# Constants in written order, the first batch's keys turned by TensorE, fillers at the end, and new instruction sequences

## The chip, the cores and the metric

The kernel runs on one core of one Trainium2 chip. The metric is device time in microseconds (us), the median of three runs. Five engines work beside each other: TensorE (PE) multiplies matrices, VectorE (DVE), ScalarE (ACT) and GpSimd (POOL) work on tiles element by element, and SyncE (SP) issues most of the DMA transfers. Each engine takes its instructions strictly in the order in which they were written for it. So an instruction that waits holds up everything queued behind it on its engine. Matrix products land in PSUM, everything else lies in SBUF.

## What is computed

Four batches of 12288 queries attend to pooled keys. The keys and values are one array: kv, averaged over 4 x 4 patches and multiplied by w_sr, 768 rows of 128 per batch. The 49152 rows that come out go through a layer of 8 experts, of which each row takes the one with the largest gate logit.

```
kv_pool = kv.reshape(B, H//r, r, W//r, r, C).mean(axis=(2, 4))     # r = 4
k = v = kv_pool.reshape(B, -1, C) @ w_sr
s = scale * (q @ k.T);  a = softmax(s);  x = a @ v
e = argmax(x @ w_gate);  p = softmax(x @ w_gate)[e]
out = p * (relu(x @ w1[e]) @ w2[e])
```

## The kernel before

**Blocks.** The rows are worked in 96 blocks of 512 queries, 24 to a batch (`block(t)`, from L1125). A block first makes three pairs of score products on PE (tile `s`, "scores"). For each pair ACT makes the exponential (L1166, tile `e`) and DVE the difference 1 + s - exp(s) (L1168, tile `r`). Then PE makes four groups of "values" (tile `po`): r times the keys in tile `v16`, and the query times the square M of the keys, which makes up for the terms taken out of r. The result goes, split into two half-precision parts, through a DMA transpose to tile `x`. The expert's products follow: `hidden` (x times `w1U`, tile `b`), ACT's relu, and `rows` (x times `L` and g times `w2U`), DVE's scaling by the gate (L1297, tile `y`) and the store.

**Keys.** `keys(b)` (from L528) makes a batch's keys. For the first batch kv is loaded by SP in 8 transfers of 512 KB and 8 of 256 KB; DVE adds pairs of rows ("joins", L603 and, for the last third, L565), PE sums the rest and turns it (the products `s<-ident,kv`, "key sums"), multiplies by w_sr, and ACT writes `vT` (keys down the partitions). From `vT` come the scaled keys `KT` for the scores, the centred keys `kt` (L698), and two turned copies: `v16`, and `kr` as a high and a low half-precision part. Here POOL makes the halves (L712, L714) and the copy `kp2` (L706), and SP turns them by two DMA transposes (L716 into `kr`, shown as PU, and L708 into `v16`). `square` multiplies `kr` by itself for M; nothing of the values can start without M and v16. The loads of the first batch borrow the buffers of `e`, `raw` and `r`.

**Expert.** `expert(b)` (from L748) guesses the batch's expert from the mean key, loads its two weight matrices and folds, sorts and packs them in a long chain over all engines that starts from the square of the keys (`Ms`). `hidden` and `rows` need its results w1U, zb, L and w2U. Until then blocks can only do scores and values.

**Constants.** Before all this some dozens of small tiles are made by DVE and POOL (L400 to L469). The counting row `iota_i` is made by POOL in a buffer called `e2`, the third buffer of `e`. These lines stand outside `tc.manual_schedule()`, so their place among the other instructions is chosen by the framework and not by the order in the file.

**Order.** All other work is handed to a planner (`Plan`, `op`, `order`, `issue`) as ops with an engine, an estimated duration and what they need and give. The order on each engine is written out by hand as lists of op numbers (`ORDER`), and `WAYS` chooses between variants of an op that different engines can do. The planner's estimated times decide two things only: which buffer an op gets, and where PE gets "fillers". A filler is three products of the constant `slots16` with itself (128 x 384 each) into a free PSUM bank, of no use for the result; it is put where the planner sees PE idle between 9 and 110 us.

**General steps.** After each of the first three batches a step with loads, a search and an indirect gather (`general_step`) is mixed in among the blocks; a loop at the end runs as many more as are left.

Of the kernel before, what the change touches and what calls it, by code (L numbers as in the profile page):

```python
# [17 lines left out]
P = 128  # L18
POOL = 4
# [65 lines left out]
PE 1 0 2 4-5 3 6-7 9-10 8 11 110 12 112 14 98-99 113 111 101 100 16 13 145 21 144 15 17 146 115-117 114 122-123 103 102  # L85
104-105 124 148 22 18 147 149-150 133 24 135 126 23 125 134 127-128 155 157 138-139 19 136 156 137 29 20 166 30 158-159 167
161 160 28 168 26 179 25 27 178 119 118 170 177 129 120 172 171 188 130 169 189 121 131 190 182 108 107 181 183 180 106 199
151 201 132 193 153 200 191-192 210 194 152 109 211 140 212 205 204 31 141 221 32 202-203 184 162 222-223 143 142 213-214
232 216 173 215 234 154 233 163 224 185 227 226 225 243 164 186 244 235 237 236 245 238 206 255 195 33 256 249 34 246 254
187 248 174 265 175 247 35 266 165 176 260 196 267 259 207 258 257 197 276 198 278 269 208 218 270-271 277 217 268 209 37  # L90
# [3 lines left out]
359 358 399 307 297 50 377 51 388 316 48 390 317 49 401 383 308 327 381 328 400 318 380 382 319 410 389 338 329 405 403-404  # L94
402 412 360 411 339 391-392 394 393 421 330 423 416 414 422 361 413 415 341 432-433 362 427 424-425 349 426 384 52 434 443
53 363 350 437 340 444 435 385 364 436 445 351 438 395 456 352 396 454 447-448 446 455 386 449 467 387 406 465 417 365 458
466 407 460 397 457 459 478 408 477 398 470 428 476 468 419 469 471 54 499 418 409 55 498 429 481-482 430 368 487 480 489
# [3 lines left out]
516 557 61-63 517 577 569 528 567 570 576 518 568 586 519 540 587 578 529 538 588 581 67 597 580 579 527 539 599 591 589 598  # L101
590 592 610 68 64 601 530 69 609 608 602 550 603 549 600 70 619-620 551 541 612 561 611 560 621 630 562 552 613-614 631 573
563 632 65 623-624 654 571 622 572 625 66 655 582 656 633 636 635 665 583 634 574 666 73-74 593 667 72 657 584 659 594 658
689 71 687 660 585 688 604 670 668 605 671 669 595 678 596 615 676 607 606 698 691 617 677 692-693 690 637 699 616 700 628
681 627 680 682 679 618 639 710 709 704 638 701 75 703 626 711 76 720 640-641 702 673 629 732 722 661 683 712-713 662 721
# [5 lines left out]
794 856 858 795 857 863 785 796 806 886 867 875 804 91 805 876 87 868 866 816 869 92 887 817 885 807 815 879-880 93 838 877  # L111
896 878 818 898 891 827 889 897 88 826 890 888 828 89 909 908 837 829 900 848 901 931-932 850 840 902 95 899 907 839 94 933
96 849 954 860 911-912 861 910 913 97 953 859 851 870 935 942 937 871 955 881 872 934 936 944 862 964 892 873 943 957 882
965 883 959 903 893 958 956 966 884 946-947 975 945 894 948 976 895 977 969 916 967 970 905 968 914-915 988 986 904 978 981
938 979 918 917 987 980 939 906 940 997 999 991-992 961 960 989 998 990 962 1019 941 1020 949 963 1010 919 1000 1009 1002
951 1003 950 1008 971 1001 993 973 1021 952 1030 1012 1011 972 983 1013-1014 1032 984 1031 1024 982 1025 1022 922 920 1041
974 1043 1023 921 995 1042 1033 1065 1036 994 1034-1035 1004 1063 985 1064 1044 996 1052 1045 1054 1047 1005 923 1046 1006
924 1017 1053 1069 1066 1007 1016 925 1074 1015 1067 1075 1068 926 1076 1057-1058 927 929 1056 1085 1055 1018 1080 1086 1070
# [6 lines left out]
ACT 0 2-3 1 4 6 5 7 112 9 114 10 8 103-104 115 113 106 105 14 19 11 18 12 138 137 13 139 116-117 121-122 21 108 107 20 123  # L125
15 22 140 128 141 130 16 129 124 17 145 147 23 132 146 28 131 152-153 29 148 27 154 25 162 24 133 26 161 118-119 160 125 120
168 156 126 155 169 127 170 110-111 163 109 175 142 177 176 144 182 143 171 183 134 184 30 135 189 31 178 165 149 164 191
190 197 136 157 185 199 150 198 166 192 204 151 205 167 206 200 179 212 32 213 33 211 172 158-159 219 207 193 220 173 221
# [226 lines left out]
def attention_moe(ctx: ExitStack, tc, q, kv, w_sr, w_gate, w1, w2, out):  # L355
# [90 lines left out]
    for i, n in enumerate(LIMITS):  # L446
        nc.vector.memset(limits[:, i:i + 1], float(2 * n - F + 1))
# [1283 lines left out]
```

## Time and profile before

| | |
|---|---|
| median of three runs | 735.5 us (734.69, 735.5, 737.92) |
| the profiled execution | 739.06 us, of which its span is 737.3 us |
| PE / DVE / ACT / POOL busy | 96% / 85% / 82% / 74% |
| products on PE, of them fillers | 7903, 66 |
| granted TensorE clock over the span | 0.995 |

The span runs from the first to the last instruction. The share of busy time is an average: the stages at the start, where PE waits for the first keys, and at the end look different from the middle. Matrix products are pipelined, so the shown time of one is longer than the distance from one to the next.

### The profile page before, as it was taken

To read this page: it belongs to the slowest core of one execution; us is meant where nothing else is said; L and a number is where in the kernel's file an instruction comes from. 1 tells how busy PE (TensorE), PEld (TensorE's weight loads), DVE (VectorE), ACT (ScalarE), POOL (GpSimd) and SP (SyncE) were. 2 spreads that over 40 slices of the span, in tenths; PEclk is the share of its full clock that TensorE was granted. 3 is DMA by queue.
4 is the path that set the end of the run, shared out by engine and by line. 5 is a ranking of instruction groups with operands and counts; after the bars stand their busy time and mean duration, and the time that the engine had idled before them with its cause. 6 is when DMAs were issued, how large, how long until landed. Compare 5 with 4: busy or idle time off the path is not lost.

```text
span 737.3 us, 20803 instructions
## 1 busy us (share of the span) xinstructions
PE 705.2 (96%) x7903; PEld 555.2 (75%) x7903; DVE 626.0 (85%) x1257; ACT 607.4 (82%) x1118; POOL 544.8 (74%) x777
## 2 busy tenths in 40 slices
PE   4999999999999998999999999999999999999995
PEld 4677777888777777787877777888877877877773
DVE  5679879889998997888998898898988899777874
ACT  0567888999888996889978888889989898798972
POOL 0376899886889878677778879878676787668752
PEclk9999999999999999999999999999999999999998
DMA  8797899995899999789789999979787899877532
GB/s 315 207 248 125 207 206 224 186 206 130 175 252 232 238 243 211 152 212 186 131 205 220 208 253 222 189 164 223 146 155 170 167 188 186 177 154 157 99 91 73
DMA packets 326757, 138.84 MB, mean 188 GB/s; under 512 B 212558, under 2 KB 318162, under 8 KB 326656
## 3 DMA queue, kind: packets, MB, share of 16 engines
q1 hardware_dynamic: 325904, 137.14, 85.3%
q8 instruction: 62, 1.02, 0.6%
q14 instruction: 39, 0.32, 0.1%
q10 hardware_dynamic: 560, 0.20, 0.1%
q0 software_dynamic: 192, 0.17, 0.1%
HBM read 59.12 MB, written 26.94 MB: 117 GB/s over the span
## 4 chain that ended last, share of the span: by engine, by line
PE 79%; DVE 9%; ACT 5%; DMA 3%; issue 2%; POOL 1%; SPq 0%; DVEq 0%; ACTq 0%; POOLq 0%
PE b L477 36%; PE po L477 24%; PE s L477 17%; DVE r L1168 4%; ACT e L1166 2%; DMA x<-xp 1%; ACT g L1272 1%; DVE xp L1203 1%; DMA kv<-in_kv_dram 1%; DVE y L1297 1%; DMA qT<-qp 1%; PE s L876 0%; ACT xp L1202 0%; POOL g L1262 0%; PE s L838 0%
## 5 line engine op out<-in xcount | busy, mean ns | idle before, releaser
L1168 DVE SCALAR_TENSOR_TENSOR r<-s,e 128x1024 bf16<-128x1024 f32 x288 | 346.0, 1215 | 38.8 <-ACT e L1166 37.0
L1166 ACT ACTIVATE e<-s 128x1024 f32<-128x1024 f32 x288 | 293.4, 1029 | 38.4 <-PE s L477 34.3
L477 PE MATMUL po<-v,r 128*128 128x145 f16 x2304 | 254.2, 228 | 2.5 <-DVE xp L1203 1.7
L477 PEld LDWEIGHTS <-r 128*128 128x128 bf16 x2304 | 168.2, 98 | 22.7 <-DVE xp L1203 1.6
L477 PE MATMUL s<-qT,KT 128*128 128x512 f16 x576 | 168.0, 379 | 5.7 <-DVE r L1168 3.7
L477 PE MATMUL b<-x,w1U 128*128 128x512 f16 x465 | 142.6, 379 | 3.0 <-DVE y L1297 2.6
L1272 ACT ACTIVATE g<-b,zb 128x512 f16<-128x512 f32 x185 | 128.0, 694 | 17.4 <-PE b L477 16.2
L477 PE MATMUL po<-M,qT 128*128 128x136 f16 x1152 | 131.5, 223 | 0.0
L477 PE MATMUL b<-w2U,g 128*128 128x128 f16 x1180 | 129.7, 220 | 0.0
L1264 POOL TENSOR_TENSOR g<-X,g 80x512 f16<-80x512 f32 x94 | 108.8, 1159 | 26.0 <-ACT g L1272 8.8
L477 PE MATMUL b<-L,x 128*128 128x128 f16 x1116 | 123.7, 220 | 1.6 <-DVE X L1252 1.3
L1149 POOL TENSOR_TENSOR qp<-qr,qp 128x512 f16<-128x512 f32 x94 | 108.7, 1161 | 13.5 <-DVE PU L939 3.5
L477 PEld LDWEIGHTS <-qT 128*128 128x128 f16 x1152 | 84.9, 98 | 30.0 <-issue 5.5
L477 PEld LDWEIGHTS <-x 128*128 128x128 f16 x1116 | 81.6, 98 | 18.1 <-issue 2.4
L1147 POOL CAST qp<-qr 128x512 f16<-128x512 f32 x94 | 57.1, 614 | 36.6 <-DVE r L565 22.2
L477 PEld LDWEIGHTS <-g 128*128 128x128 f16 x1180 | 82.9, 99 | 0.2 <-DVE g L1255 0.2
L1262 POOL CAST g<-X 128x512 f16<-128x512 f32 x94 | 57.5, 612 | 28.8 <-PE b L477 9.0
L477 PEld LDWEIGHTS <-KT 128*128 128x128 bf16 x576 | 51.1, 99 | 35.1 <-issue 11.8
L618 POOL TENSOR_TENSOR kv<-kv,kv 128x512 f32<-128x512 f32 x54 | 68.1, 1276 | 10.0 <-DMA kv<-in_kv_dram 3.7
L1297 DVE TENSOR_TENSOR y<-b,gt 128x512 f32<-128x512 f32 (+1 forms) x97 | 65.5, 678 | 8.6 <-PE b L477 4.7
L1260 ACT ACTIVATE X<-b,zb 128x512 f32<-128x512 f32 x94 | 65.1, 695 | 7.1 <-PE b L477 6.2
L477 PEld LDWEIGHTS <-w1U 128*128 128x128 f16 x480 | 45.6, 99 | 31.6 <-issue 2.4
(380 smaller groups left out, 921.5 us busy)
## 6 DMA issues: line engine op xcount, KB each, us to landing
qr<-in_q_dram SPq DMA_DIRECT2D x96, 256.0 KB, 3.4
out_dram<-y SPq DMA_DIRECT2D x95, 256.0 KB, 3.2
kv<-in_kv_dram SPq DMA_DIRECT2D x41, 512.0 KB, 5.7
raw<-in_moe_w_dram SPq DMA_DIRECT2D x14, 512.0 KB, 4.9
e<-in_kv_dram SPq DMA_DIRECT2D x3, 512.0 KB, 6.5
v_dram<-vT SPq DMA_DIRECT2D x4, 384.0 KB, 4.1
qT<-qp SPq DMA_TRANSPOSE x94, 3.9
x<-xp SPq DMA_TRANSPOSE x91, 3.9
```

The lines of the kernel that those rows point to most:

```text
L477: return nc.tensor.matmul(o, l, r, start=start, stop=stop)
L618: nc.gpsimd.tensor_add(flat(to), flat(to), flat(of))
L1147: op("POOL", .62, lambda: nc.gpsimd.tensor_copy(qp.tile[:, 0], qr.tile), T - 1.9 * LEN, [("qr", t)], [("qh", t)], [qr, qp])
L1149: op("POOL", 1.17, lambda: nc.gpsimd.tensor_sub(qp.tile[:, 1], qr.tile, qp.tile[:, 0]), T - 1.8 * LEN, [("qh", t)], [("qp", t)], [qr, qp])
L1166: op("ACT", 1.03, lambda e=e, ps=ps: nc.scalar.activation(e.tile, ps.tile, AF.Exp), at + .6, [("s", t, s)], [("e", t, s)], [ps, e])
L1168: op("DVE", 1.22, lambda e=e, ps=ps, s=s: nc.vector.scalar_tensor_tensor(r.tile[:, 2 * s:2 * s + 2], ps.tile, 1.0, e.tile, op0=ALU.add, op ...
L1203: op("DVE", .69, lambda: nc.vector.tensor_tensor(xp.tile[:, 1], po.tile[:, :, :C], xp.tile[:, 0], op=ALU.subtract), A + .5, [("xh", t)], [ ...
L1260: op("ACT", .69, lambda ph=ph, zu=zu: nc.scalar.activation(gf.tile, ph.tile, AF.Relu, bias=zu()), at + .5, [("ph", t, u), ("zb", b)], [("g ...
L1262: op("POOL", .62, lambda: nc.gpsimd.tensor_copy(gg.tile[:, 0], gf.tile), at + 1.5, [("gf", t)], [("gh", t), ("g", t)], [gf, gg])
L1264: op("POOL", 1.16, lambda: nc.gpsimd.tensor_sub(gg.tile[:PAIRS, 1], gf.tile[:PAIRS], gg.tile[:PAIRS, 0]), at + 2, [("gf", t), ("gh", t), ( ...
L1272: op("ACT", .78, lambda u=u, ph=ph, zu=zu: nc.scalar.activation(gg.tile[:, u], ph.tile, AF.Relu, bias=zu(), accum_out=k["fl"].tile[:, u - ...
L1297: nc.vector.tensor_tensor(y.tile[:, cs], py.tile.rearrange("p (c d) -> p c d", d=C)[:, cs], bc(gr["gt"].tile[:, 0, js], C)[:, cs], op=ALU. ...
```

## The change

Five things change.

1. The constants are put inside `tc.manual_schedule()`: they are issued in the order in which they are written, ahead of all the planner's work. No constant is added or taken away.
2. For the first batch the two turned copies are made by PE instead of DMA. `turn` transposes `vT` and `kt` by six products each into PSUM; ACT copies the one, scaled, into `v16` and the other into the high half of `kr`; DVE subtracts for the low half. POOL's three ops and SP's two transposes of this batch are gone. The other three batches keep the old way.
3. Fillers are allowed in two stretches of planned time: 9 to 110 us as before, and 690 to 800 us.
4. The planner's estimate of the 256 KB loads goes from 0.64 to 0.73 us.
5. All five lists of ORDER are new, and WAYS differs in 58 names. On PE there are two more ops (the turns), on DVE five more, on ACT as many as before, on POOL seven and on SP two fewer. Of the 96 blocks, 91 instead of 89 leave out the third part of `rows` (u); 20 instead of 22 give the split of x to POOL rather than DVE (x); 33 instead of 32 copy the logits on DVE (l); KT's second third goes from ACT to DVE (k1).

The first numbers of the lists, old and new, decoded: on DVE of before the joins start with op 2 (rows 0 and 1 of the first third), of after with ops 0 and 1 (the gate weights' scale), then 3 (rows 2 and 3), then 2. On PE of before the key sum of rows 0 and 1 (op 1) is first and the gate weights' product (op 0) second; of after the gate weights come first, then the sum of rows 0 and 1, then that of rows 2 and 3. On PE of after `turn` of vT is 13, `turn` of kt 14, `square` 15, the gate guess 16, the logits' product 17, the expert's first products 18 and 19; blocks 0 and 1 start at 100 and 112 (98 and 110 before). On DVE of after 181 and 176 are the query halves of blocks 1 and 0, 182 to 184 and 177 to 179 their `r`, 201 one of block 4; 18 is KT, 19 and 20 are kt, 21 the subtraction for kr, 22 M's low half, 23 to 25 the expert guess, 26 the logits.

```diff
 ORDER = turns("""
-PE 1 0 2 4-5 3 6-7 9-10 8 11 110 12 112 14 98-99 113 111 101 100 16 13 145 21 144 15 17 146 115-117 114 122-123 103 102
+PE 0-2 4-5 3 6-7 9-10 8 11 112 13 114 12 100 16 101 115 14 113 103 15 147 17-18 102 23 119 117 146 118 116 19 105 148 104
...
-DVE 2 0 3 5 1 6 8-10 12 7 13 4 11 14-16 179 17 21 18 22 19 181 174-175 182 180 177 176 23 20 42 199 24 198 25-26 200 183 27
+DVE 0-1 3 2 5-6 8-10 12-13 7 4 11 15 14 18 16 181 17 183 23 19 24 20 177 184 176 21 182 25 179 22 201 26 44 178 200 185
...
-SP 3 0-1 4 2 5 7 6 10 14 8 12 9 11 13 15 82 71 94 68 74 83 78 86 19 17 16 21 20 98 110 90 75 22 102 18 23 87 79 72 106 95 91
+SP 3 1-2 0 5 4 7 6 10 12 8 14 11 9 15 13 72 69 80 76 66 73 84 92 81 17 88 18-19 21 20 100 112 16 104 77 70 96 85 93 82 89 74
...
-            if o.eng == "PE" and self.filler and start < self.filler_end:
+            if o.eng == "PE" and any(lo < free["PE"] and start < hi for lo, hi in self.filler_times):
                 make, fill, us = self.filler
-                while free["PE"] > self.filler_start:
+                while True:
...
-    ident = keep("ident", [P, P])
-    make_identity(nc, ident)
+    with tc.manual_schedule():
+        ident = keep("ident", [P, P])
+        make_identity(nc, ident)
...
+        if b == 0:
+            back = {}
+            for name, of, needs in (("tv", vT, [("vT", b)]), ("tk", kt, [("kt", b)])):
+                to = back[name] = pair()
+
+                def turn(to=to, of=of):
+                    flat = to.tile.rearrange("p b x -> p (b x)")
+                    for t in range(KT):
+                        nc.tensor.transpose(flat[:, t * P:(t + 1) * P], of.tile[:, t * P:(t + 1) * P], ident)
+
+                op("PE", .68, turn, at + 3, needs, [(name, b)], [of, to])
+            keys_of = lambda n: back[n].tile.rearrange("p b x -> p (b x)")[:, :NK].rearrange("p (t c) -> p t c", c=P)
+            op("ACT", .83, lambda: nc.scalar.activation(v16.tile[:, :, :P], keys_of("tv"), AF.Copy, scale=cn[:, 11:12]), at + 4,
+               [("tv", b), ("rest", b)], [("v16", b)], [back["tv"], v16])
+            op("ACT", .83, lambda: nc.scalar.copy(kr.tile[:, 0], keys_of("tk")), at + 4.5, [("tk", b)], [("kr0", b)],
+               [back["tk"], kr])
+            op("DVE", .95, lambda: nc.vector.tensor_tensor(kr.tile[:, 1], keys_of("tk"), kr.tile[:, 0], op=ALU.subtract), at + 5,
+               [("kr0", b)], [("kr", b)], [back["tk"], kr])
+        else:
...
-    plan.filler, plan.filler_start, plan.filler_end = (bank().make, fill, .487), 9.0, 110.0
+    plan.filler, plan.filler_times = (bank().make, fill, .487), ((9.0, 110.0), (690.0, 800.0))
```

## Rows read from the trace of the kernel before

**Rows 1.** Busy time of PE, PEld, DVE, ACT, POOL; granted clock; DMA, in stretches.

```profile
500.00:600.00 100.00, 100.00 (x1187) 79.63 (x1185) 89.49 (x168) 90.47 (x168) 74.96 (x114) 1.00 0.87 170
715.00:737.30 22.30, 12.72 (x142) 9.87 (x139) 11.29 (x49) 6.76 (x16) 6.81 (x19) 0.90 0.20 60
```

**Rows 2.** The page's chain that ended last, by engine.

```profile
PE 79%; DVE 9%; ACT 5%; DMA 3%; issue 2%; POOL 1%; SPq 0%; DVEq 0%; ACTq 0%; POOLq 0%
```

**Rows 3.** Timeline of the first sums: start, length, engine, line, tiles, what was awaited.

```profile
8.30 1.22 DVE L603 TENSOR_TENSOR kv<-kv,kv 128x1024 f32<-128x1024 f32 x1 [6.18 <-DMA kv<-in_kv_dram]
...
9.67 3.75 PE L477 MATMUL s<-ident,kv 128*128 128x128 f32 x16 [9.67 <-DVE kv L603]
...
15.60 3.86 PE L477 MATMUL s<-ident,kv 128*128 128x128 f32 x32
```

**Rows 4.** What SP's queue waited for before 60 us: total, times, longest.

```profile
SPq L545 <- DVE slot L431: 5.1, 1, 5.1
```

**Rows 5.** Busy time in two stretches, with the DMA rate (GB/s) last.

```profile
9.00:12.00 3.00, 2.33 (x11) 2.36 (x12) 3.00 (x27) 0.00 (x0) 0.00 (x0) 1.00 1.04 415
12.00:15.00 3.00, 2.94 (x14) 2.06 (x14) 2.96 (x8) 0.00 (x0) 0.00 (x0) 1.00 0.89 288
```

**Rows 6.** Timeline from the centred keys to the first values, and L716's landing.

```profile
30.89 0.54 DVE L698 TENSOR_SCALAR kv<-vT,con 128x512 f32<-128x512 f32 x1
...
34.15 2.71 SPq L716 DMA_TRANSPOSE PU<-kv  x1
...
40.54 1.17 PE L477 MATMUL b<-PU 128*128 128x128 f16 x18
...
49.04 0.23 PE L477 MATMUL po<-v,r 128*128 128x145 f16 x1
...
DMA to landing us min/median/max: 5.1/5.1/5.1
```

**Rows 7.** Busy time in three stretches of the start.

```profile
28.00:40.00 12.00, 10.16 (x57) 5.49 (x57) 10.54 (x20) 7.74 (x10) 8.11 (x12) 1.00 0.96 214
40.00:46.00 6.00, 5.74 (x50) 3.97 (x47) 2.78 (x13) 5.30 (x10) 3.16 (x5) 1.00 1.02 312
46.00:60.00 14.00, 13.28 (x147) 11.66 (x147) 12.77 (x22) 8.12 (x13) 8.61 (x14) 1.00 0.92 183
```

**Rows 8.** Groups by line, 28 to 60 us: count, busy, mean ns, idle before.

```profile
L1168 DVE SCALAR_TENSOR_TENSOR r<-s,e 128x1024 bf16<-128x1024 f32 x11 | 13.4, 1219 | 1.0 <-ACT e L1166 0.8
L477 PE MATMUL b<-slots 128*128 128x384 f16 x45 | 9.3, 325 | 0.2
L838 PE MATMUL s<-ident,raw 128*128 128x128 f32 x8 | 1.1, 279 | 0.3 <-DVE r L1168 0.3
L845 ACT COPY kv<-s 128x1024 f32<-128x1024 f32 x1 | 1.0, 1012 | 0.8 <-PE s L838 0.8
L841 DVE TENSOR_TENSOR kv<-s,kv 128x768 f32<-128x768 f32 x1 | 1.0, 959 | 0.0
```

**Rows 9.** First and last products with w1U: count, ns, first and last start.

```profile
L477 PE MATMUL b<-x,w1U x465: 376/379/634, 82.1 to 724.2; 128*128 128x512 f16 x155
```

**Rows 10.** Busy time in a stretch of the end (clock third from last).

```profile
727.00:730.00 3.00, 2.73 (x34) 2.67 (x33) 1.25 (x6) 0.00 (x0) 0.00 (x0) 0.63 0.02 5
```

**Rows 11.** Chain that ended last, at the end.

```profile
725.96 3.25 PE b L477 x32
...
729.46 1.53 PE b L477 x25
```

**Rows 12.** PE's longest wait from 720 us on: total, times, longest.

```profile
PE b L477 <- DVE X L1252: 1.3, 1, 1.3
```

**Rows 13.** Busy time around the slowest stretch of the middle.

```profile
265.00:280.00 15.00, 13.89 (x155) 10.60 (x154) 13.26 (x24) 11.48 (x23) 10.05 (x15) 1.00 1.10 232
280.00:295.00 15.00, 13.56 (x143) 10.81 (x143) 11.94 (x21) 10.69 (x17) 14.79 (x16) 0.89 1.15 236
```

**Rows 14.** Chain that ended last, in that stretch.

```profile
271.96 8.90 DMA x<-xp
```

More of the change, by code (lines that the diff above doesn't have):

```diff
@@ L246, in __init__ @@
     def __init__(self, slots):
-        self.ops, self.slots, self.filler, self.filler_start, self.filler_end = [], slots, None, 0.0, 0.0
+        self.ops, self.slots, self.filler, self.filler_times = [], slots, None, ()
     def op(self, eng, us, fn, at, needs=(), gives=(), bufs=(), lands=0.0, moves=0.0, lock=False, way=None):
@@ L411, in attention_moe @@
-    col_i = keep("col_i", [P, NF], I32)
-    nc.gpsimd.iota(col_i, pattern=[[P, NF]], base=0, channel_multiplier=1)
-    iota_e = keep("iota_e", [P, E])
-    lists = keep("lists", [P, NL])
-    nc.vector.tensor_scalar_add(lists, iota_i[:, :NL], 1.0)
-    nc.vector.tensor_scalar_add(iota_e, iota_i[:, :E], float(-E))
-    slots16 = keep("slots16", [P, UN], F16)
-    own_at, used_at = OWN_U * P + OWN_AT, P + PAIRS
-    for lo, hi, n in ((0, P, 1), (P, used_at, USED + 1), (used_at, own_at, P + 1),
-                      (own_at + OWN, 2 * P, P + 1 + own_at - used_at), (2 * P, UN, RU - P + 1)):
-        nc.vector.tensor_scalar_add(slots16[:, lo:hi], iota_i[:, lo:hi], float(n - lo))
@@ L422, in attention_moe @@
-    nc.vector.memset(slots16[:, own_at:own_at + OWN], -1.0)
-    wg_raw = keep("wg_raw", [P, E])
-    wsr = keep("wsr", [P, C])
-    wg_st = keep("wg_st", [P, 4])
-    code = keep("code", [P, NJ + 1])
-    nc.vector.memset(code, 0.0)
-    left, steps = keep("left", [P, NL]), keep("steps", [P, NL])
-    nc.vector.memset(left, 0.0)
-    slot = keep("slot", [P, P + 1])
-    nc.vector.tensor_copy(slot, iota_i[:, :P + 1])
-    part_i = keep("part_i", [P, 1], I32)
-    nc.gpsimd.iota(part_i, pattern=[[0, 1]], base=0, channel_multiplier=1)
@@ L434, in attention_moe @@
-    part_col = keep("part", [P, 1])
-    nc.vector.tensor_copy(part_col, part_i)
-    own = keep("own", [P, UH + OWN])
-    nc.vector.memset(own, 0.0)
-    for i in range(OWN):
-        nc.vector.tensor_scalar(own[:, UH + i:UH + i + 1], part_col, float(OWN_AT + i), None, op0=ALU.is_equal)
-        nc.vector.scalar_tensor_tensor(own[:, OWN_U:OWN_U + 1], own[:, UH + i:UH + i + 1], OWN_ONE, own[:, OWN_U:OWN_U + 1],
-                                       op0=ALU.mult, op1=ALU.add)
-    rare = keep("rare", [P, P])
@@ L452, in attention_moe @@
-    nc.vector.tensor_copy(band, band_i)
-    band1 = keep("band1", [P, 1])
-    nc.vector.tensor_scalar_add(band1, band, 1.0)
-    for t in range(KT):
-        nc.vector.tensor_scalar(extra[:, t, 1:], slots16[:, :NG], band1, -1.0, op0=ALU.is_equal, op1=ALU.mult)
-    below = keep("below", [P, P])
-    nc.vector.tensor_scalar(below, slot[:, :P], part_col, None, op0=ALU.is_gt)
-    below_b = keep("below_b", [P, P], BF16)
-    nc.vector.tensor_copy(below_b, below)
-    step = keep("step", [P, 1])
@@ L551, in load @@
                                 ap=[[POOL * W * C, HB // 3], [2 * POOL * C, WB // 2], [1, POOL * C]]))
[L552 removed]
+                    move = (.73 if halves else KV_MOVE[b > 0]) + (KV_FIRST if b == 0 and d == 0 and i < 3 else 0.0)
                     op("SP", .6, load, at + (i / 4 if a is None else a * 2 + i / 4), follow, [("kv", b, d, i) if a is None else ("kv", b, d, i, a)], [raw],
@@ L700, in keys @@
                [("unit", b), ("vT", b)], [("kt", b), ("kt", b, n)], [vT, kt], lock=True)
-        kp, kp2, kr = buf("kv", [P, 2, NK], F16), buf("junk", [P, NK], F16), buf("PU", [P, 2, KT, P], F16)
-        v16 = k["v16"] = buf("v16", [P, KT, XR], F16)
-        op("ACT", .92, lambda: nc.scalar.activation(kp2.tile, vT.tile, AF.Copy, scale=cn[:, 11:12]), at + 4,
-           [("rest", b), ("vT", b)], [("kp2", b)], [kp2, vT], way=(f"a{b}", 0))
-        op("POOL", .93, lambda: nc.gpsimd.tensor_scalar(kp2.tile, vT.tile, cn[:, 11:12], 1.0, op0=ALU.mult, op1=ALU.mult),
-           at + 4, [("rest", b), ("vT", b)], [("kp2", b)], [kp2, vT], way=(f"a{b}", 1))
@@ L708, in keys @@
-        op("SP", 1.35, lambda: nc.sync.dma_start_transpose(v16.tile[:, :, :P], kp2.tile), at + 5, [("kp2", b)],
-           [("v16", b)], [kp2, v16], lands=2.0, moves=1.2)
-        op("ACT", .83, lambda: nc.scalar.copy(kp.tile[:, 0], kt.tile), at + 4.5, [("kt", b)], [("kp0", b)], [kt, kp],
-           way=(f"b{b}", 0))
-        op("POOL", .92, lambda: nc.gpsimd.tensor_copy(kp.tile[:, 0], kt.tile), at + 4.5, [("kt", b)], [("kp0", b)], [kt, kp],
-           way=(f"b{b}", 1))
-        op("POOL", 1.66, lambda: nc.gpsimd.tensor_sub(kp.tile[:, 1], kt.tile, kp.tile[:, 0]), at + 5, [("kp0", b)],
-           [("kp1", b)], [kt, kp])
```

347 lines of the change are left out of this document (206 added, 141 removed), and 47 rows, old and new, of the table ORDER.

## Prediction

> **What bounds the kernel now.** I read the busy times by stretch first. From 500 to 600 us PE is busy all the time, with DVE and ACT at 90% [rows 1], and the chain that ended last lies on PE for 79% of the span [rows 2]. So the middle is set by PE, with two engines close behind, and the kernel's end is the start of this full stretch plus the work that is then left for PE. Time can be won where PE does nothing useful: before 82 us, where the expert's first products start [rows 9], and at the end, where it is busy for 12.72 of 22.3 us [rows 1]. That is where four of the five changes lie. The fifth, new sequences for everything, has no row of its own.
>
> The profiled execution took 739.06 us, 1.76 us more than its span, and the median of the three runs is 735.5 us, 3.56 us less. I make the sum on 739.06 us and take 3.56 us off at the end.
>
> **First sums.** Before, DVE joined its first pair at 8.30 us, when its loads had landed, then made the remaining constants, and PE's first key sum ran from 9.67 for 3.75 us; the second could start only at 15.60 [rows 3]. PE filled the 2.2 us between 13.42 and 15.60 with the gate weights and fillers. The late constants also held up the loads: `iota_i` lies in a buffer of `e`, so SP's queue waited 5.1 us, until DVE had read it for `slot` [rows 4], and the DMA rate fell from 415 to 288 GB/s for 3 us [rows 5]. That is 0.38 MB, or 0.9 us at the full rate, by which all later loads can now land earlier.
>
> After, the constants lie in the idle time before 8.30 us, where DVE waits for the load for 6.18 us [rows 3], and cost nothing. But the lists change what PE waits for: DVE now joins rows 2 and 3 first, while PE's first sum is still that of rows 0 and 1. So it waits for a second join of 1.22 us [rows 3] and starts near 10.9. Its 3.75 us end at 14.65, and the second sum then follows without a gap, against 15.60: **1.0 us won**. From there on PE was busy before (2.94 of 3 us from 12 on [rows 5]), so the earlier loads bring no more. Bounds: if the second sum also goes at the pace of the first (3.75 us, not half of 3.86 [rows 3]), 0.9 us is lost; if PE doesn't start later, 2.2 us is won.
>
> **Turning the first keys.** Before, kt was ready at 31.43; POOL's two ops and SP's transpose (2.71 us on SP, 5.1 us to landing) came between it and `square` at 40.54, and the first values started at 49.04 [rows 6]: 9.1 us and 17.6 us behind kt. In their place come six turns, an ACT copy and a DVE subtraction. Eight turns took 1.1 us, ACT's copy of 1024 columns 1.0 and a DVE operation on 768 columns of PSUM 0.96 [rows 8], so the new path is about 0.8 + 0.8 + 0.96 = 2.6 us. The list puts other work in between: one `r` before kt, two more and a query half before the subtraction. With 1.22 us for each `r` [rows 8] and half as much for the query half that is 4.3 us. So `square` starts some 7 us behind the old place of kt and 2 us earlier than before; with the two `r` ahead of M's low half, the logits' product and the last `r`, I expect the first values near 43 us.
>
> What is this worth at the end? Not 6 us, for the scores and values of this stage hang on DVE. DVE idled for 1.46 us from 28 to 40, 3.22 us from 40 to 46 and 1.23 us from 46 to 60 [rows 7]; the hole from 40 to 46 is the wait for M and v16, with the three buffers of r full. Closing it and half a microsecond of the next gives 4.0 us, less what DVE gets anew: the subtraction, 0.96 us [rows 8], and KT's second third, at most the 0.54 us of a larger tile of kt [rows 6]. **2.5 us won.** Bounds: none of the holes closed and the new work paid, 1.5 us lost; all 5.9 us closed, 4.4 us won.
>
> PE pays for the turns: twelve, or 1.6 us at the pace of the eight [rows 8]. The cover is the 15 fillers (45 products, 9.3 us of busy time) between 28 and 60 [rows 8], and it costs nothing as long as they are there; otherwise 1.6 us. The Trainium skill (TensorE: Matmul & The Clock Gate, Part 4: PE-mode transpose) speaks against it: a turn of this size costs about 275 ns in a kernel. By that price twelve would be 3.3 us; the row shows 0.14 us apiece, as they are pipelined (its mean of 279 ns is the latency of one).
>
> POOL and SP lose work that stood ahead of others: 2.71 us on SP [rows 6] ahead of the next keys' loads. The second batch's keys are needed only after 24 blocks, so this is worth nothing by itself.
>
> **The end.** From 727 to 730 us the granted clock was 0.63 [rows 10], after PE had waited 1.3 us for DVE [rows 12] and more before it. On the chain 32 products took 3.25 us there, where 25 of the same kind a little later took 1.53 [rows 11], which is 61 ns each; at that pace 32 take 1.95 us, so the slow clock costs 1.3 us. Fillers in the gaps can keep the clock. **1.0 us won**, since the gaps must fit them. Bounds: 1.3 won; or a filler is in the way when the awaited work comes. A filler takes about 0.5 us (three products of 128 x 384, priced from the pace of 61 ns for 128 columns), and at three such places that is 1.5 us lost.
>
> **The sequences.** Two more blocks without their third part of `rows` save 8 products, 0.5 us at 61 ns [rows 11]. The rest can't be read from this trace, and its sign is open. Its size has a row: from 265 to 295 us PE idled for 2.55 us, and a clock of 0.89 over 15 us cost another 1.65 [rows 13], behind a DMA transpose of 8.9 us on the chain [rows 14]. One such stall more or less is 4.2 us. I put the rest at zero, since nothing shows a side, and keep 4.2 us either way for the range.
>
> **Sum.** 739.06 - 1.0 - 2.5 - 1.0 - 0.5 = 734.06 us for a profiled execution, **730.5 us** for the median. The change is 5.0 us; 0.5%, about what a measurement can tell from no change here, is 3.7 us (731.8 to 739.2 us counts as the same).
>
> **Rivals.**
> *The expert, not the values, sets the start.* The full stretch begins with w1U at 82 us [rows 9]. Its chain starts from the expert guess, which the list now puts behind an `r` of 1.22 us, and its loads stand on SP behind two transposes that wait for POOL. If w1U comes no earlier, the earlier values only fill buffers, and the 2.5 us are not won: 735.5 - 2.5 = 733.0 us. For it: nothing of the chain itself is shorter. Against: its first products need the square of the keys, which comes earlier.
> *The stall in the middle goes.* The loads of the general step and the transposes meet in another order, and the 4.2 us are not repeated: 726.3 us. For it: one piece of DMA of 8.9 us stands alone in this chain. Against: the same loads must still pass one queue.
> *Slower: more such stalls.* SP's single queue carries loads, stores and transposes, and an x that lands late leaves PE without values and then at half clock. There are three general steps and three loads of keys that can meet so. Each costs 4.2 us; two more leave 730.5 + 8.4 = 738.9, which is no change, and from three on it is slower: 743.1 us. For it: all lists are new, and the planner's times decide buffers only. Against: no more than one stall of this size stands in the trace.
> *The change doesn't do what it says:* the constants don't end before 8.30 us, as DVE waits in written order for POOL's rows. Then the first sums stay where they were: 731.5 us, within the forecast.
>
> **How the numbers follow.** The forecast, with its own range of 727 to 734 us, gets 0.50, of which 0.37 lies below 731.8; the expert as the bound 0.19; the lost stall 0.15; more stalls 0.16. Faster by over 0.5% is 0.37 + 0.15 = 0.52, the same 0.13 + 0.19 = 0.32, slower 0.16. The range goes from 723 us (the lost stall with the upper ends of the first sums and the keys, not all at once) to 740 us (one stall more, with nothing won: 735.5 + 4.2).
>
> **What would show it.** Right: SP without the wait for `slot`; PE's first sum near 10.9 us and no filler before the second; `square` by 39 us and first values near 43; DVE idle under 1.5 us where it idled 3.2; w1U's first product by 79.5 us; the clock near 1 after 720 us. Wrong: values earlier but w1U still at 82 us (the first rival); PE idle or a clock under 1 at new places between 110 and 715 us (stalls); fillers on the chain at the end.

## Result and profile after

| | before | after |
|---|---|---|
| median | 736.42 us (20 executions) | 729.50 us (20 executions) |
| ratio of after to before | | 0.9909, 95% interval 0.9891 to 0.9927 |
| the profiled execution | 739.06 us, span 737.3 | 728.98 us, span 727.2 |
| granted clock over the span | 0.995 | 0.999 |

The change makes the kernel 6.9 us faster. The two profiled executions differ by 10.1 us, which is more than the change is worth: that of before lies 2.6 us above its median, that of after 0.5 us below.

The chain that ended last is still PE's, with a smaller share than before [rows 2]:

```profile
PE 71%; DVE 13%; ACT 7%; issue 4%; DMA 3%; POOL 1%; SPq 0%; DVEq 0%; ACTq 0%; POOLq 0%
```

**First sums.** PE's timeline of after: start, length, engine, line, operation, what was awaited. It answers [rows 3]: one row of sums where there were two with fillers between them.

```profile
11.24 7.65 PE L478 MATMUL s<-ident,kv 128*128 128x128 f32 x48 [7.80 <-DVE band L455]
18.72 1.95 PE L478 MATMUL s<-ident,e 128*128 128x128 f32 x16
...
23.46 1.06 PE L478 MATMUL s<-ident,r 128*128 128x128 f32 x8
24.36 1.02 PE L478 MATMUL b<-pT,wsr 128*128 128x128 f32 x4
```

From 11.24 us on PE goes from one sum to the next without a pause, and its last products with w_sr, which end the key sums, start at 24.36 us. Before, they started at 25.03:

```profile
25.03 1.02 PE L477 MATMUL b<-pT,wsr 128*128 128x128 f32 x4
```

A difference of 0.67 us also lies between executions of the same first sums. In the three other kernels of this document that have those of before (turn_only, old_start180, old_start) these products start at 24.97, 24.36 and 24.02 us; in the six that have those of after (turn_undone, new_start180, old_end, sub_twice, new_start, end_fill) at 24.91, 24.53, 23.99, 23.94, 23.91 and 23.56 us. The means, with before and after themselves, are 24.60 and 24.17. So the first sums win some 0.4 us, which is less than either group is wide.

DVE's timeline shows why the sum starts where it does:

```profile
8.61 1.23 DVE L604 TENSOR_TENSOR kv<-kv,kv 128x1024 f32<-128x1024 f32 x1 [3.11 <-DMA kv<-in_kv_dram]
9.76 0.15 DVE L453 CAST band<-band_i 128x1 f32<-128x1 int32 x1
9.86 1.23 DVE L604 TENSOR_TENSOR kv<-kv,kv 128x1024 f32<-128x1024 f32 x1
11.01 0.15 DVE L455 TENSOR_SCALAR band<-band 128x1 f32<-128x1 f32 x1
```

Not all constants come ahead of the planner's work, as the first of the five changes has it: on DVE a few stand between the joins (`band` here, others up to 16.6 us). SP's longest waits before 60 us no longer hold one for `slot` [rows 4]; the short ones at the line of the key loads wait for earlier loads. In the stretch from 12 us the DMA rate (last column) is 397 GB/s instead of 288 [rows 5], and DVE's last join starts at 20.47 us instead of 23.30; the sums don't gain as much, since PE is busy with those before it:

```profile
SPq L550 <- DMA kv<-in_kv_dram: 2.6, 3, 1.1
```
```profile
12.00:15.00 3.00, 3.00 (x17) 3.00 (x16) 2.21 (x9) 0.00 (x0) 0.00 (x0) 1.00 1.03 397
```

**Turned keys.** The timelines of PE, ACT and DVE, against [rows 6]: the two turns, ACT's copies, DVE's subtraction, the square, and the first values at 41.84 us instead of 49.04.

```profile
25.70 0.82 PE L713 MATMUL s<-ident,vT 128*128 128x128 f32 x6
29.91 0.91 ACT L717 ACTIVATE v<-s,con 128x768 f16<-128x768 f32 x1
31.54 0.54 DVE L699 TENSOR_SCALAR kv<-vT,con 128x512 f32<-128x512 f32 x1
33.33 0.87 PE L713 MATMUL s<-ident,kv 128*128 128x128 f32 x6
34.24 0.80 ACT L719 CAST PU<-s 128x768 f16<-128x768 f32 x1 [1.31 <-PE s L713]
35.08 0.96 DVE L721 TENSOR_TENSOR PU<-s,PU 128x768 f16<-128x768 f32 x1
36.52 1.17 PE L478 MATMUL b<-PU 128*128 128x128 f16 x18
41.84 0.22 PE L478 MATMUL po<-v,r 128*128 128x145 f16 x1
```

Busy time in the stretches of [rows 7] (PE, PEld, DVE, ACT, POOL, then clock, DMA share, GB/s). DVE's, the third, is the one to read: in the middle stretch 4.49 us are busy, where 2.78 were.

```profile
28.00:40.00 12.00, 11.16 (x76) 6.68 (x76) 11.25 (x26) 9.13 (x14) 6.81 (x12) 1.00 0.75 217
40.00:46.00 6.00, 5.70 (x63) 4.95 (x63) 4.49 (x11) 5.26 (x10) 4.04 (x4) 1.00 1.06 376
46.00:60.00 14.00, 13.59 (x141) 10.89 (x141) 13.08 (x22) 10.31 (x14) 10.22 (x15) 1.00 0.63 118
```

Products with w1U (count, shortest, median and longest ns, first and last start) begin at 78.7 instead of 82.1 us and none is slow [rows 9]. The fillers: 33 products instead of 66, and the last starts at 63.0 us, so **the second stretch for fillers received none**.

```profile
L478 PE MATMUL b<-x,w1U x465: 376/379/390, 78.7 to 717.7; 128*128 128x512 f16 x155
```
```profile
L478 PE MATMUL b<-slots x33: 322/326/326, 28.0 to 63.0; 128*128 128x384 f16 x33
```

**The end**, against [rows 10 to 12]: PE's waits from 700 us on (total, times, longest), and the last products on the chain. What was 32 products in 3.25 us and 25 in 1.53 is now 57 in 3.38.

```profile
PE b L478 <- DVE X L1273: 1.4, 2, 1.1
PE b L478 <- DVE x L1246: 0.7, 1, 0.7
PE b L478 <- ACT g L1293: 0.6, 1, 0.6
```
```profile
717.71 3.38 PE b L478 x57
```

**The middle**, against [rows 1, 13]. The full stretch is as full as before. PE's gaps lie at 250 and at 340 us, and no stretch of 15 us has a clock under 1.

```profile
250.00:265.00 15.00, 13.38 (x160) 10.54 (x158) 13.85 (x34) 12.68 (x27) 10.76 (x15) 1.00 0.94 194
...
340.00:355.00 15.00, 13.29 (x140) 10.20 (x137) 14.36 (x22) 13.13 (x20) 9.59 (x15) 1.00 0.76 134
500.00:600.00 100.00, 99.89 (x1189) 78.63 (x1188) 89.35 (x179) 91.06 (x167) 75.65 (x111) 1.00 0.83 169
```

**How far ahead at 110 us.** PE's busy time and products up to 110 us and behind it; first before, then after:

```profile
0.00:110.00 110.00, 95.31 (x890) 1.00 0.86 218
110.00:738.00 628.00, 609.94 (x7016) 0.99 0.86 183
```
```profile
0.00:110.00 110.00, 94.78 (x911) 1.00 0.83 227
110.00:728.00 618.00, 600.97 (x6964) 1.00 0.87 183
```

At 110 us PE has 52 products less ahead of it. From 110 to 250 us, where it is busy all the time, one product of the mixture takes 85 ns (139.49 us for 1635), so that is 4.4 us. Eight of them, 0.5 to 0.7 us, are the third parts of `rows` that two more blocks leave out; **some 3.8 us are the lead that PE has by then**, the new order up to 110 us included.

### The profile page after: what moved, and what is told of

The parts are those of the page before. It is cut to its first block, busy times and chain, and to the rows that moved or that the text cites. A ratio compares the mean times of both kernels' runs of the same rounds, so it can differ in the third digit from the quotient of the medians.

```text
span 727.2 us, 20777 instructions
## 1 busy us (share of the span) xinstructions
PE 695.8 (96%) x7874; PEld 548.7 (75%) x7874; DVE 632.3 (87%) x1262; ACT 609.2 (84%) x1120; POOL 538.4 (74%) x770
## 3 DMA queue, kind: packets, MB, share of 16 engines
q1 hardware_dynamic: 323536, 136.55, 85.6%
## 4 chain that ended last, share of the span: by engine, by line
PE 71%; DVE 13%; ACT 7%; issue 4%; DMA 3%; POOL 1%; SPq 0%; DVEq 0%; ACTq 0%; POOLq 0%
PE b L478 31%; PE po L478 22%; PE s L478 16%; DVE r L1189 6%; ACT e L1187 3%; DMA kv<-in_kv_dram 2%; DVE y L1318 1%; DMA x<-xp 1%; ACT g L1293 1%; ACT X L1281 1%; DVE xp L1224 1%; ACT xp L1223 0%; DVE junk L1428 0%; PE s L859 0%; PE s L1588 0%
## 5 line engine op out<-in xcount | busy, mean ns | idle before, releaser
L1293 ACT ACTIVATE g<-b,zb 128x512 f16<-128x512 f32 x187 | 129.3, 694 | 11.5 <-PE b L478 10.9
```

What stands on the lines that cost most here:

```text
L1293: op("ACT", .78, lambda u=u, ph=ph, zu=zu: nc.scalar.activation(gg.tile[:, u], ph.tile, AF.Relu, bias=zu(), accum_out=k["fl"].tile[:, u - ...
```

## Experiments

Theory A is the prediction's: the start carries most of the gain, by the first sums and by the earlier values. Its rival B: the new sequences of the middle and the end carry it. The other letters stand in the expectations. All ratios are to the kernel before, on the same chip.

| kernel | median us | ratio, 95% interval | last products with w_sr, us | first product with w1U, us | between the two, us |
|---|---|---|---|---|---|
| before | 736.42 | 1 | 25.03 | 82.1 | 57.1 |
| the change | 729.50 | 0.9909 (0.9891 to 0.9927) | 24.36 | 78.7 | 54.3 |
| consts_only | 736.59 | 1.0006 (0.9983 to 1.0029) | 24.40 | 81.4 | 57.0 |
| consts_loose | 731.98 | 0.9937 (0.9917 to 0.9958) | 25.00 | 79.3 | 54.3 |
| pair_first | 728.89 | 0.9907 (0.9871 to 0.9943) | 24.43 | 78.7 | 54.3 |
| turn_only | 742.93 | 1.0078 (1.0048 to 1.0109) | 24.97 | 85.6 | 60.6 |
| turn_undone | 739.38 | 1.0033 (1.0015 to 1.0051) | 24.91 | 90.3 | 65.4 |
| sub_twice | 730.88 | 0.9925 (0.9897 to 0.9954) | 23.94 | 79.3 | 55.4 |
| new_start | 739.35 | 1.0037 (1.0014 to 1.0061) | 23.91 | 78.2 | 54.3 |
| old_start | 735.19 | 0.9987 (0.9966 to 1.0007) | 24.02 | 81.0 | 57.0 |
| new_start180 | 733.80 | 0.9968 (0.9947 to 0.9989) | 24.53 | 78.9 | 54.4 |
| old_start180 | 734.57 | 0.9971 (0.9951 to 0.9992) | 24.36 | 81.4 | 57.0 |
| old_end | 732.67 | 0.9951 (0.9931 to 0.9970) | 23.99 | 78.3 | 54.3 |
| end_fill | 728.88 | 0.9870 (0.9843 to 0.9896) | 23.56 | 77.9 | 54.3 |

The last column is the steadiest number of this table. When the key sums end differs by up to 1.35 us between kernels whose first sums are the same; from there to the first product with w1U it is 57.0 or 57.1 us in all four kernels that have the old turning in the lists made for it, and 54.3 or 54.4 us in all seven that have the new turning in its own. So **the turned keys, with the lists made for them, bring w1U 2.7 us forward**.

### The constants

consts_only is before with this; consts_loose is after without it:

```diff
-    ident = keep("ident", [P, P])
-    make_identity(nc, ident)
+    with tc.manual_schedule():
+        ident = keep("ident", [P, P])
+        make_identity(nc, ident)
...
```

> The kernel before with its constants inside the written order and nothing else (part 1 alone; its first join stands ahead of the constants on DVE). Theory A: the constants need the lists of the change to bring anything, as DVE's written order puts the first join ahead of them: 736.4 us, not more than 0.5 us faster, and the wait of SP's queue stays. Rival C (the constants' place alone frees the loads): SP's wait is gone and the time falls by 1 us to 735.4.

> The changed kernel with its constants outside the written order again (part 1 undone, all else kept). Before: the kernel at 736.4 us, changed 729.5. Theory A (the prediction's): the order of the constants is worth the wait of SP's queue and 1 us of PE's first sums, so the time rises by about 1 us to 730.5, and SP waits again some us for DVE. Rival B: the gain lies in the new sequences from 60 us on, and the constants are worth nothing: 729.5 within 0.5 us.

Alone the constants are worth nothing that the times show (1.0006, 0.9983 to 1.0029). SP's longest wait is still the one for `slot`, first of consts_only, then of consts_loose:

```profile
SPq L546 <- DVE slot L432: 5.9, 1, 5.9
```
```profile
SPq L545 <- DVE slot L431: 5.2, 1, 5.2
```

Written order frees SP's queue only if the joins are not written ahead of the readers of `iota_i`, and before's list of DVE begins with a join. That part of theory A holds. In consts_loose PE's first sum starts at 12.17 us (11.24 in the change), its last products with w_sr at 25.00 (24.36), w1U's at 79.3 (78.7): 0.6 us late, all of it in the first sums and no more than these differ by in the same code. In the same way consts_only ends its key sums 0.6 us ahead of before (24.40), although SP still waits. The time of consts_loose is 2.1 us above that of the change by the ratios, 2.5 by the medians, with intervals that overlap. So the time leans to A and the size isn't settled; 1.6 us of the profiled execution lie in the clock at its end, which "The end" below takes up.

### PE's own pair first

The first loads on SP and the first joins on DVE are those of the pair that PE sums first:

```diff
-DVE 0-1 3 2 5-6
+DVE 0-1 2-3 5-6
-SP 3 1-2 0 5 4
+SP 0-1 3 2 5 4
```

> The changed kernel with two entries of DVE's list and two of SP's exchanged: the pair of rows that PE sums first is loaded and joined first. Theory A: PE's first sum starts at about 9.9 us and not at 11.2, but the later sums wait for their own loads and joins, so 0.3 to 1 us of it is left at the first score products: 728.5 to 729.2. Rival G (the loads set the pace, the last join is as late as before): 729.5 within 0.3 us.

```profile
8.40 3.75 PE L478 MATMUL s<-ident,kv 128*128 128x128 f32 x16 [4.95 <-DVE band L453]
11.95 2.46 PE L478 MATMUL b<-slots 128*128 128x384 f16 x9
14.25 1.95 PE L478 MATMUL s<-ident,kv 128*128 128x128 f32 x16
...
24.43 1.02 PE L478 MATMUL b<-pT,wsr 128*128 128x128 f32 x4
```

PE's timeline shows the first sum 2.8 us earlier and the last product no earlier. By the time (0.6 us less by the medians, the same ratio) A and G can't be told apart; by the trace nothing is left at w1U, as G has it. Its last join is also as late as G says (20.59 us, 20.47 in the change), but PE doesn't wait for it: it ends at 21.28, and PE's sum of it starts at 23.53, behind the other sums. What held them up stands earlier: the second join ended at 11.22 us, and PE started its sum at 14.25, behind three fillers (nine products). The planner's estimate of the loads put them there, and they took what the pair had won. Without fillers between the sums this kernel was not run.

### The turned keys

turn_only puts the new lines of `keys` into before and adds the turns to its lists; turn_undone puts the old lines back into after:

```diff
-        kp, kp2, kr = buf("kv", [P, 2, NK], F16), buf("junk", [P, NK], F16), buf("PU", [P, 2, KT, P], F16)
...
+        if b == 0:
+            back = {}
+            for name, of, needs in (("tv", vT, [("vT", b)]), ("tk", kt, [("kt", b)])):
...
```

> The kernel before with the first keys turned by TensorE and nothing else (part 2 alone, in the order of before). Theory A: the square of the keys starts some 3 to 4 us earlier than at 40.5, but the list of before puts the expert's first products ahead of it and the general order of the rest was made for other times: between 1 us faster and 1 us slower than 736.4. Rival D (turning alone carries the gain, whatever the order): 2.5 us faster or more, 733.9 or less. Rival E: an order that is fitted to other times is lost by the edit, and stalls in the middle and the end make it slower by 2 to 4 us.

> The changed kernel with the first keys turned by POOL and DMA as before, in the order of the change (part 2 undone). Theory A: the square waits again until about 41 us, the first values until about 46 to 49, and with nothing else in PE's list ahead of them the time rises by 2.5 to 4 us to 732 to 733.5. Rival B (the sequences of the middle and the end carry the gain, the start is absorbed): 729.5 to 730.5.

Both missed by far: turning alone costs 5.7 us (1.0078), and taking it back costs 9.1 us (1.0033 against 0.9909). PE's timelines of turn_only and of turn_undone:

```profile
34.70 2.60 PE L483 MATMUL b<-slots 128*128 128x384 f16 x15
37.30 0.87 PE L718 MATMUL s<-ident,vT 128*128 128x128 f32 x6
...
43.46 1.17 PE L483 MATMUL b<-PU 128*128 128x128 f16 x18
```
```profile
35.44 11.37 PE L485 MATMUL b<-slots 128*128 128x384 f16 x69
47.55 1.18 PE L485 MATMUL b<-PU 128*128 128x128 f16 x18 [0.74 <-DMA PU<-kv]
```

In turn_only the list has the turn of vT among the score products. It needs one of the two pairs of score banks in PSUM, so PE fills 2.6 us until one is free, DVE waits 1.8 and 2.0 us for exponentials of late scores, and the square comes at 43.46, later than with the DMA (40.54). In the change the turn of vT stands at 25.70 us, ahead of all scores. In turn_undone POOL makes the halves behind work for queries and has them 3.4 us later than before, and the transpose then stands on SP for 5.85 us (2.71 before); so the square waits for the keys until 47.55 us, not 40.54, and with it next in its list PE can do nothing but fill for 11.4 us. Each list that I adapted thus added a delay of its own, and neither run prices the turns by themselves; rival E has the sign of turn_only. They show two other things. The first product with w1U moves by 3.5 and 11.6 us, and the time follows by 5.7 (3.5 to 8.0 by its interval) and 9.1: a delay of the start isn't absorbed later. And an edit to the keys needs lists made for it.

### DVE's new work, doubled

```diff
-            op("DVE", .95, lambda: nc.vector.tensor_tensor(kr.tile[:, 1], keys_of("tk"), kr.tile[:, 0], op=ALU.subtract), at + 5,
+            op("DVE", .95, lambda: [nc.vector.tensor_tensor(kr.tile[:, 1], keys_of("tk"), kr.tile[:, 0], op=ALU.subtract)
+                                    for _ in range(2)], at + 5,
```

> The changed kernel with DVE's subtraction for the low half of the turned keys made twice (0.96 us more on DVE at 36 us, the same result). Theory A (DVE sets the start, each microsecond that it gets anew between 28 and 60 us is paid): 0.9 to 1.3 us slower than the change, 730.4 to 730.8. Rival H (DVE's holes or PE's fillers take it up): the same as the change within 0.3 us.

It came out 1.2 us above the change by the ratios and 1.4 by the medians. That is where A puts it, but the interval (0.9897 to 0.9954) holds the change's own ratio, so the times don't exclude H. The trace does, up to w1U:

```profile
23.94 1.02 PE L478 MATMUL b<-pT,wsr 128*128 128x128 f32 x4
```
```profile
L478 PE MATMUL b<-x,w1U x465: 376/379/390, 79.3 to 719.7; 128*128 128x512 f16 x155
```

Between the two lie 55.4 us, where all seven kernels with the single subtraction have 54.3 or 54.4, so the 0.96 us are paid in full. The square is late by as much: 13.17 us behind the same products, 12.16 in the change. The subtraction stands on the way to the square, so this prices work on that path; that any work on DVE between 28 and 60 us is paid isn't shown by it.

### Start and rest

Four kernels join the code and order of one kernel's start with the order of the other's rest, at about 100 or 180 us of planned time; old_end has before's order for the last 90 us only. The lists are those of the two kernels, joined there; the head of PE's list in new_start180 against before:

```diff
 ORDER = turns("""
-PE 1 0 2 4-5 3 6-7 9-10 8 11 110 12 112 14 98-99 113 111 101 100 16 13 145 21 144 15 17 146 115-117 114 122-123 103 102
...
+PE 0-2 4-5 3 6-7 9-10 8 11 112 13 114 12 100 16 101 115 14 113 103 15 147 17-18 102 23 119 117 146 118 116 19 105 148
...
```

> The changed kernel's code and its order up to about 100 us, with the order of the kernel before for all that comes later (the third part of rows and the other variants too). Theory A (the start carries the gain: first sums 0.7, turning and earlier values 2.5 or more): 3 to 4 us faster than before, 732.4 to 733.4. Rival B (the new order of the middle and the end carries it): 736.4 within 1 us. If both carry half, this and the run with the halves exchanged add up to the 6.9 us.

> The kernel before (constants outside the written order, first keys turned by POOL and DMA) with its own order up to about 100 us and the order of the change for the rest. Theory A: 3 to 4 us faster than before, that is slower than the change by what its start carries: 732.4 to 733.4. Rival B (the middle and the end carry all of the gain): 729.5 to 730.5.

Joined at 100 us the new start loses 2.7 us (1.0037) and the old start gains 1.0 (0.9987): neither theory. The joint is itself a cost, probably since the two orders hold different blocks open there; that reason is argued and not shown. PE's busy time behind the joint, in new_start:

```profile
100.00:120.00 20.00, 18.34 (x203) 13.50 (x201) 14.33 (x20) 15.73 (x29) 16.82 (x20) 1.00 0.90 215
120.00:140.00 20.00, 19.16 (x227) 14.68 (x226) 17.05 (x32) 17.05 (x33) 17.08 (x25) 1.00 0.79 167
```

PE idles for 2.5 us, where it idled for 0.25 before. So the joint was moved into the full stretch:

> As the run with the new start, but the two orders are joined at about 180 us of planned time and not at 100, since PE idled for some 2.6 us just behind the earlier joint. The changed kernel's code and order up to there (that is, up to the full stretch), the order of the kernel before behind it. Theory A (the start carries a lead of 4 us that PE then keeps): 3 to 4.5 us faster than before, 732.2 to 733.7. Rival B' (an order is fitted to the times that led up to it, and the old rest gives the lead back in stalls at its loads and general steps): 0 to 2 us faster, 734.7 to 736.7, with more PE idle between 180 and 460 us than either kernel shows.

> The counterpart: the kernel before (its code and order) up to about 180 us of planned time, the order of the change behind it. Theory A: the rest of the change is worth what the start leaves over of 6.9 us, so 2.5 to 4 us faster than before, 732.5 to 734. Rival B': as the run joined at 100 us, about 1.5 us faster only, 735. If the lead of this one and that of its counterpart add up to 6.9 us, the two halves are independent; if they add up to less, the rest is that the orders fit each other.

Now the new start wins 2.4 us (0.9968), the new rest 2.1 us (0.9971), 4.5 of 6.7 together. Each interval is about 1.5 us wide to either side, so the two may well add up to the whole; what is left over can't be told from joints that still cost something. In new_start180 PE idles for 7.5 us from 180 to 460 us, 6.3 in before and 6.4 in after: the sign that B' named, some 1.2 us. A and B both get a part: the start is the larger part by PE's products at 110 us (3.8 us), and **the rest isn't zero**. Part 4 of the change and the new WAYS have no run of their own.

> The changed kernel until about 640 us, with the order of the kernel before for the last 90 us. Theory A: at the end the change only loses the gaps that let the clock fall (1.3 us by the chain of before) and a wait of 1.3 us: 1 to 2 us slower than the change, 730.5 to 731.5, with a granted clock well under 1 in the last 15 us. Rival F (the order of the end is worth nothing, its clock followed from work that came earlier): 729.5 within 0.5 us, clock near 0.93 at the end.

old_end is 3.1 us slower than the change by the ratios, more than A said; 1.5 us of that is PE's idle time at its joint, from 640 to 700 us. Its clock from 715 us to its end is 0.71 in the profiled execution, whose mean over the span (0.994) is one of the three lowest of twelve; the mean of the twelve, 0.9968, is not below the change's 0.9964.

### The end

In the change PE's waits of 0.72, 0.65 and 1.09 us stand in front of the last 57 products. The same waits, to 0.01 us, stand there in consts_loose and old_start180, which have the same order at the end. The chain's step of the 57 products in sub_twice, consts_loose and old_start180:

```profile
719.66 3.38 PE b L478 x57
```
```profile
718.81 5.00 PE b L477 x57
```
```profile
721.61 6.15 PE b L485 x57
```

In old_start180 the granted clock from 721 to 727 us is 0.50, the lower level (1.2 GHz), and the products take twice as long in part. So whether the clock falls here is not settled by the order alone, and what it costs is 1.6 to 2.8 us. By the mean clock over the whole span the two kernels can't be told apart: 0.9965 over the 90 executions of before that stood beside these kernels and 0.9964 over the 20 of after. But that mean doesn't say where the clock fell. The profiles do: in the last 15 us of PE's work the granted clock is 0.77 or 0.89 in all six with before's end (before, consts_only, turn_only, new_start, new_start180, old_end), the same in four of the seven with the change's (consts_loose, turn_undone, old_start, old_start180), and 1.00 in the other three (after, pair_first, sub_twice). With one profile of each kernel, whether the new order keeps the clock more often stays open.

Why did the planner place no filler in these gaps? By the code, PE waits there until a bank of the pool that the expert's products write is cleared, and this pool has two (`PSUM = {"s": 2, "po": 1, "b": 2}`). A filler takes a bank of the same pool, so it fits nowhere. In end_fill single products go into the score banks, which stand empty by then:

```diff
+            for _ in range(self.ahead.get(o.gives[0], 0) if o.gives else 0):
+                i = min(range(len(slots["s"])), key=lambda i: slots["s"][i])
...
+    plan.ahead = {("ph", 92, 2): 3, ("ph", 95, 0): 3, ("ph", 95, 2): 5}
```

> The changed kernel with fillers at its end after all: single products of 128 x 384 (0.16 us each) in front of the three operations of PE that wait longest there, three ahead of the waits of 0.72 and 0.65 us and five ahead of that of 1.09 us, into the score banks of PSUM, which stand empty by then. Theory C (the clock at the end falls by chance, in part of the executions, with the same waits in front of it, and costs 1.6 to 2.8 us of the last 57 products when it falls): the mean granted clock of the executions rises from 0.9964 to 0.998 or more, the 57 products take 3.4 us, and the median falls by 0.5 to 1 us to 728.5 to 729. Rival I (the clock of a stretch this short doesn't matter for the end, or the fillers stand in the way): 729.5 or up to 0.5 us more, with the mean clock as before.

```profile
716.05 1.08 PE L488 MATMUL s<-slots 128*128 128x384 f16 x5
717.28 0.38 PE L488 MATMUL b<-x,w1U 128*128 128x512 f16 x1 [0.15 <-DVE X L1283]
```

By these rows of PE's timeline 0.15 us are left of the wait of 1.09. On the chain the 57 products take 3.37 us, and the clock of the six executions is 0.997 to 0.999, mean 0.998, where eight of the 20 of after are at 0.995 or below. Twelve of those 20 are at 0.997 or above; six such in a row come by chance about one time in twenty. Theory C's numbers are met, rival I's are not. The time is 0.6 us lower than that of the change by the medians and 2.9 us by the ratios, as before took 738.23 us beside it; the intervals overlap narrowly (0.9896, 0.9891). So the runs agree with the mechanism, and what it is worth is open between these two.

## Why the prediction was right, and where it was not

The median came out at 729.5 us, forecast was 730.5. By steps:

**First sums: right that the loads come earlier, sized too high.** SP's wait is gone, PE starts after a second join and then goes without a gap. The two profiles give 0.67 us instead of 1.0, the groups of the same first sums some 0.4 (24.60 and 24.17 us), within their spread. So the size of this term isn't settled, and no run shows that it is the gap between the sums that cost the time. The start is 0.34 us later than the 10.9 that I took, since the first load landed 0.3 us later and a constant stands between the joins. That the constants end before 8.30 us was wrong, and cost little.

**Turning the first keys: right in size at w1U, by a reading that was in part wrong.** The square by 39 (36.52), values near 43 (41.84), w1U by 79.5 (78.7) all came, and from the end of the key sums to w1U 2.7 us are won, where 2.5 were forecast. The first rival, the expert as the bound, falls with that. But the working doesn't carry the 2.5. The hole of 3.22 us and half a microsecond are 3.7 us and not 4.0, so the terms make 2.2. And the hole from 40 to 46 us was only for 0.9 us a wait for M. Most of the rest is this wait of DVE in before (total, times, longest):

```profile
DVE ws L962 <- PE b L477: 2.0, 1, 2.0
```

It waited for a product for the expert's scales, which PE made at 44.18 us, after ACT's squares of the expert's weights (to 43.15). The buffers of `r` weren't full: by the code the three hold a block each, which is nine `r`, and eight were made before the first values. In after the same wait is 0.7 us. DVE idled 3.2 us from 28 to 60 instead of 5.9, so 2.7 us were closed there; the new work took 0.96 and 0.34 us. That is 1.4 us, and the step failed in where it stopped counting. DVE is busier also from 80 to 110 us, 25.48 against 23.94. By 110 us it has made 38 `r` where before it had made 35, and three of 1.22 us are 3.7 us. First sums and turning, with the lists made for them, are the 3.8 us of PE's lead at 110 us, 3.5 were forecast. How much of it the turns would bring in other lists isn't shown.

That the twelve turns cost nothing fits the rows: 0.82 and 0.87 us for six, 0.14 apiece, and 33 filler products fewer. The Trainium skill (TensorE: Matmul & The Clock Gate, Part 4: PE-mode transpose) has some 275 ns for one in a kernel. The trace agrees with that for the time of one, 272 ns; but each of these starts before the one ahead of it is done, so twelve take 1.69 us and not 3.3.

**The end: the step failed.** No filler was placed. In the two profiles the last 57 products did become 1.4 us faster, which looks like the forecast 1.0 us, but with the same order at the end they took 5.00 to 6.15 us in four other profiles. The fillers are worth nothing in the change; whether the new order of the end is, stays open. What the step overlooked is where a filler's bank comes from.

**The sequences: put at zero, they are worth about 2 us.** 0.5 us for fewer third parts of `rows` stands, and old_start180 measures 2.1 us (0.6 to 3.6) for all that comes behind 180 us. Where the other 1.6 us lie isn't settled. The 4.2 us of the stall [rows 13, 14] were no fixed cost either: in consts_only, with before's lists, PE's clock is 1.00 from 250 to 300 us, and it idles 2.26 us there against 2.66 in before.

So the sum held by luck in part, since errors met: 1.0 us counted for the end and some 0.6 for the first sums that did not come, and some 1.6 that came from the rest. Of the other rivals, the lost stall (726.3 us) was not reached. The fourth came in half: not all constants end before 8.30 us, but SP's wait is gone. Slower by new stalls, the third, was not seen: PE's idle time between 110 and 700 us is 7.2 us after and 7.8 before.

## What to carry to other kernels

In a kernel whose engines run lists written by hand, the worth of an edit at the start is read from how much work is left for the bounding engine once it is full (here 52 products less at 110 us), and the lists must be made for the edit: the same lines in lists made for other times cost 5.7 us, where in their own they bring w1U 2.7 us forward. A stage is best measured from its own beginning: the end of the key sums differs by up to 1.35 us where the code of the sums is the same, but from there to w1U kernels with the same keys agree to 0.1 us, and a difference of 1.0 us is plain that the medians can't show. A constant or a turn put early helps only if what it needs (a buffer, a PSUM bank) is free where the list puts it, and the same holds for fillers, which need a bank that the awaited work does not hold. What lies in the clock of a short stretch must not be read from one profile of each kernel.

## What the hardware showed that was not expected

- The key sums begin at half their later pace. The first sixteen products take 3.75 us and sixteen later ones 1.95, whether they begin at 9.67 us (before) or at 8.40 (pair_first), with a granted clock of 1.00 in the rows of these stretches. The pace doesn't change at the same product each time: the 48 in one row take 7.65 us in after, 7.30 in sub_twice and 8.23 in turn_undone. With the first join, which starts between 8.07 and 8.88 us in the kernels with the change's first sums, this is why the end of the sums differs between executions. Why the pace is halved isn't shown.
- The same waits of PE (0.72, 0.65 and 1.09 us) were followed by 57 products in 3.38 us (after, pair_first, sub_twice), and in 5.00, 5.01 and 6.15 us (consts_loose, turn_undone, old_start180).
- The middle isn't the same twice. PE's list of pair_first is that of after from the first values on, yet in the first of these rows (pair_first, then after) PE idles for 0.97 and 2.01 us:

```profile
250.00:300.00 50.00, 49.03 (x552) 37.86 (x549) 45.92 (x98) 43.84 (x83) 42.26 (x56) 1.00 0.96 221
```
```profile
250.00:300.00 50.00, 47.99 (x534) 36.88 (x532) 44.97 (x98) 42.59 (x82) 41.35 (x54) 1.00 1.02 219
```
